# A fused scan, expert and gated-layer kernel: silu's table load placed earlier, and work in later stages re-spaced

## The chip, the cores and the metric

The kernel runs on one core of a Trainium2 chip. The metric is the device time of one execution in microseconds (us). Engines are named as in the profile: PE (TensorE matmul), PEld (its weight loads), DVE (VectorE), ACT (ScalarE), POOL (GpSimd), SP (SyncE, which issues the DMAs).

## What is computed

A chunked linear scan gives 3072 tokens of 256 features. A mixture of 4 experts with normalised weights follows, and then one gated layer with silu:

```python
x = scan(x, a, B, C)                     # 3072 x 256 tokens
p = domain_probs / (domain_probs.sum(-1, keepdims=True) + 1e-09)
out = np.zeros((N, D), dtype=np.float32)
for e in range(E):                       # E = 4, F = 1024
    h = np.maximum(x @ w1[e], 0.0)
    out += p[:, e:e + 1] * (h @ w2[e])
g = out @ w_gate                         # d_ff = 1536
silu = g * (1.0 / (1.0 + np.exp(-g)))
val = out @ w_val
return (silu * val @ w_out)
```

## The kernel before

Every fp32 product is made of rounded parts: a value is split into a high and a low part, and three matmuls (high by high, low by high, high by low) take the place of one. A plain 128x512 product therefore shows as three rows on PE (or as two rows, one of them x2). The suffixes h and l in tile names are these parts. `high` (L702 in the trace) is ACT's copy that rounds, `low` (L705) is the subtraction on POOL that leaves the rest.

The work has four stages, and PE goes through them in one written order.

- **Scan, with experts 0 and 1 for the first 2048 tokens**, to 223 us. Slots 0 to 159 of about 1.3 us each hold half of one token tile's product with one block of w1 and w2; the scan's steps are put between them.
- **Eight blocks of the other experts' work**, 223 to 550 us. From slot 160 (`n0`) on, eight blocks of 1024 tokens, each an expert and a pair p of token tiles: `blocks = [(2, 0), (2, 2), (2, 1), (0, 2), (1, 2), (3, 0), (3, 1), (3, 2)]`. A block has four quads, a quad four slots of some 2.55 us. A block whose expert is new has its four quads' weights prepared during the block before, which is 12 quads, from about 346 to 450 us. A quad is a 2x2 block product in the manner of Strassen, with seven products instead of eight: `expert_hidden` writes the banks X, Y, Z, W in the order X A11, Y S2, W S3, Z S1, X A12, Y A22, Z S4. After X A11 ACT copies X into Y, after Y S2 it copies Y into Z (L1032, L1035), after W S3 and Z S1 it saves W and Z into SBUF (`c<-d` L1037, `c<-h` L1040), and `out` rounds the four results (L1026). `expert_project` (L1078) multiplies them by w2 two slots or more later. Operands are sums of token tiles (`token_sums`: s1, s2, s3 on POOL at L862, with the copies t3h and t24h on ACT) and sums of weight blocks (`gate_sums`, L713 to L716, on POOL).
- **The gated layer**, 550 to 813 us, in 18 steps; step i has `dense_gate(i)` and `dense_value(i)` with the same seven products each. The gate ends in silu on ACT (L1132 through `scopy`), the value multiplies it in on DVE. `plain_product` (L985, tile `dr`) and `side_product` are the products with w_out; `plain()`, `side_product` and `before(...)` stand in the functions `fill_a` and `fill_b`, which are called between products.
- **The tail**, 813 us to the end: the last products with w_out in the order of the list `order`, added on DVE (L1281) and stored from SP and ACT.

Where the work stands is set by hand. `put(slot, fn)` and `job(steps, slots)` hang a step on a slot, `spread(seq, a, b)` spaces a sequence evenly between two slots, `quad(i, j, h)` is the slot of block i, quad j, part h. At each slot PE's products are written first into the program, and the steps of that slot are written behind them, on whatever engine they use. Each engine works through its instructions in that order. So a step at an earlier slot stands further ahead in the queue of its engine; it also blocks what is behind it if its operands are late.

`expert_quad(e, j)` prepares the weights of one quad in seven steps: `load` (two DMAs from SP into `raw_q`), `high_a` and `low_a` (the first three blocks), `sums`, `high_s` (two copies on ACT), `low_s`, `low_o`. `dense_tokens(p)` makes the token sums of a pair p in six steps (i0, i1, s2, i3, s4, s5), where i3 is s3 and the copy t3h. `expert_tokens` does the same ahead of the experts. `dense_quad` turns the gated layer's weights into parts in the same way, by way of DVE and stores to DRAM. `share_load` fetches the mixture weights of a block, `hidden_load` the weights of one gated step. The last products of the last expert block (`parts`, project 21 among them) are done inside step 0 of the gated layer, by `before(...)`.

ACT has one function table at a time. In the program an `ACT_TABLE_LOAD` stands ahead of the first silu.

## Time and profile before

| what | value |
| --- | --- |
| time, median of 3 runs | 823.12 us (822.6 to 823.57) |
| the profiled execution | 823.93 us |
| its span | 822.2 us |
| PE busy | 812.7 us, 99% of the span, 4361 matmuls |
| DVE, ACT, POOL busy | 564.8, 549.2, 504.7 us |
| granted TensorE clock | 1.00 of full speed (the 2.4 GHz level) in all 40 slices |
| DMA | 129.06 MB, 157 GB/s on average |

The profiled execution has 1.7 us around its span and is 0.8 us above the median. In the timelines a row has the start, the duration, the engine, the line, the operation, output<-inputs, and in brackets the idle time of that engine before it with what ended it (given from about 0.15 us on). A matmul row lasts 0.39 us while its successor starts 0.227 us later, because matmuls overlap; a matmul that comes after a pause is 0.50 us long.

### The profile page before, as it was taken

Reading aid. Unit: us, or ns where it says so; the run is one execution under the profiler, and the core shown is the slowest. Engines: PE = TensorE matmul, PEld = TensorE weight load, DVE = VectorE, ACT = ScalarE, POOL = GpSimd, SP = SyncE. Lnnn points to the kernel's source line nnn. Section 1 sums busy time; section 2 is a strip of 40 time slices with the busy share of each in tenths; the row PEclk is TensorE's granted clock in tenths of the full one; section 3 lists DMA queues with packets and bytes.
Section 4 is the critical chain, followed back from the end, with each engine's and each line's share of the span. In section 5 each row is a group of like instructions: output and inputs, shape, how many; then the busy total and the mean of one; then the engine's idle time right before and its main releaser. Section 6 shows DMA issues by size and latency. Waiting matters only on the chain.

```text
span 822.2 us, 12888 instructions
## 1 busy us (share of the span) xinstructions
PE 812.7 (99%) x4361; PEld 671.6 (82%) x4361; DVE 564.8 (69%) x861; ACT 549.2 (67%) x1109; POOL 504.7 (61%) x527
## 2 busy tenths in 40 slices
PE   8999999999999999999999999999999999999998
PEld 7998888888778888888888888887787888888886
DVE  6877668555257756565756574736889878877777
ACT  6687776666366565767776666546577677677763
POOL 4764775434399533777897347513688568847752
PEclk9999999999999999999999999999999999999999
DMA  8864545541301336344443242363555366637651
GB/s 272 281 233 144 170 148 193 194 165 65 105 25 48 119 97 208 116 153 142 145 160 96 92 145 94 137 237 93 174 189 194 109 249 229 225 121 269 226 165 51
DMA packets 67218, 129.06 MB, mean 157 GB/s; under 512 B 6288, under 2 KB 34512, under 8 KB 67152
## 3 DMA queue, kind: packets, MB, share of 16 engines
q1 hardware_dynamic: 67008, 128.11, 46.7%
q8 instruction: 34, 0.56, 0.3%
q14 instruction: 32, 0.26, 0.1%
q10 hardware_dynamic: 144, 0.13, 0.0%
HBM read 108.41 MB, written 19.81 MB: 156 GB/s over the span
## 4 chain that ended last, share of the span: by engine, by line
PE 94%; POOL 2%; ACT 2%; DVE 1%; issue 1%; DVEq 0%; ACTq 0%; POOLq 0%
PE h L958 31%; PE h L631 11%; PE d L1078 10%; PE po L1078 10%; PE po L639 10%; PE d L958 7%; PE d L985 6%; PE o L985 3%; PE ypsum L546 1%; PE scores L475 1%; PE h L985 1%; PE ypsum L491 1%; POOL acc L862 1%; POOL xl L705 0%; PE ypsum L504 0%
## 5 line engine op out<-in xcount | busy, mean ns | idle before, releaser
L1043 DVE TENSOR_TENSOR d<-d,c 128x512 f32<-128x512 f32 x32 | 22.3, 698 | 104.1 <-ACT c L1040 104.1
L673 DVE SCALAR_TENSOR_TENSOR hl<-h,hh 128x512 fp32r<-128x512 f32 (+1 forms) x80 | 46.5, 582 | 58.9 <-ACT hh L672 58.7
L1078 PE MATMUL po<-hh,we_o 128*128 128x512 f32 x256 | 78.9, 389 | 0.5 <-DVE acc L694 0.5
L1078 PE MATMUL d<-hh,we_o 128*128 128x512 f32 x256 | 78.9, 389 | 0.0
L1027 DVE SCALAR_TENSOR_TENSOR hl<-h,hh 128x512 fp32r<-128x512 f32 x96 | 65.9, 688 | 18.2 <-PE d L1078 12.1
L672 ACT ACTIVATE hh<-h 128x512 fp32r<-128x512 f32 (+1 forms) x80 | 40.5, 508 | 55.2 <-PE h L631 54.9
L1026 ACT ACTIVATE hh<-h 128x512 fp32r<-128x512 f32 x96 | 57.0, 596 | 25.7 <-DVE h L1047 22.6
L433 ACT ACTIVATE L<-L,cum 128x128 f32<-128x128 f32 x176 | 56.1, 394 | 3.7 <-POOL L L426 3.7
L958 PE MATMUL h<-xh,wq_h 128*128 128x512 f32 x144 | 56.6, 393 | 0.6 <-ACT xh L1132 0.6
L631 PE MATMUL h<-xh,w_h 128*128 128x512 f32 (+1 forms) x160 | 56.3, 352 | 0.7 <-POOL Bw L461 0.7
L639 PE MATMUL po<-hh,w_h 128*128 128x512 f32 (+1 forms) x160 | 56.3, 352 | 0.6 <-DVE tmp L692 0.6
L1078 PEld LDWEIGHTS po<-hh,we_o 128*128 128x128 f32 x256 | 48.0, 188 | 10.8 <-ACT we_o L702 0.9
L631 PE MATMUL h<-xh,w_l 128*128 128x512 f32 (+1 forms) x160 | 55.8, 349 | 0.4 <-DVE w_l L275 0.4
L1078 PEld LDWEIGHTS d<-hh,we_o 128*128 128x128 f32 x256 | 48.1, 188 | 10.0
L958 PE MATMUL h<-xh,wq_l 128*128 128x512 f32 x144 | 56.1, 389 | 0.0
L958 PE MATMUL h<-xl,wq_h 128*128 128x512 f32 x144 | 56.1, 389 | 0.0
L639 PE MATMUL po<-hl,w_h 128*128 128x512 f32 (+1 forms) x160 | 55.6, 348 | 0.0
L639 PE MATMUL po<-hh,w_l 128*128 128x512 f32 (+1 forms) x160 | 55.5, 347 | 0.0
L631 PE MATMUL h<-xl,w_h 128*128 128x512 f32 (+1 forms) x160 | 55.5, 348 | 0.0
L958 PE MATMUL h<-xh,we_h 128*128 128x512 f32 x128 | 50.0, 391 | 0.4 <-ACT c L1040 0.3
L958 PE MATMUL h<-xh,we_l 128*128 128x512 f32 x128 | 49.8, 389 | 0.0
L1078 PE MATMUL po<-hl,we_o 128*128 128x512 f32 x128 | 49.8, 389 | 0.0
(489 smaller groups left out, 2540.6 us busy)
## 6 DMA issues: line engine op xcount, KB each, us to landing
wq_h<-wd_d SPq DMA_DIRECT2D x36, 448.0 KB
wq_l<-wd_d SPq DMA_DIRECT2D x36, 448.0 KB
L<-crow_d SPq DMA_DIRECT2D x22, 512.0 KB
bc<-in_bc_dram SPq DMA_DIRECT2D x21, 512.0 KB
wq_o<-wp_d SPq DMA_DIRECT2D x24, 384.0 KB
raw_q<-in_w_dram SPq DMA_DIRECT2D x32, 256.0 KB
wq_s<-ws_d SPq DMA_DIRECT2D x18, 384.0 KB
pbc<-probs_d SPq DMA_DIRECT2D x22, 256.0 KB
```

The costliest lines, as they stand in the source:

```text
L433: nc.scalar.activation(out=L[:, h, :], in_=L[:, h, :], func=AF.Exp, bias=cols(cum, q)[:, h:h + 1])
L475: nc.tensor.matmul(ps[:, 2 * g:2 * g + 2, :], r["Bs"][:, 2 * half + g, :], r["Cs"][:, 2 * half + g], start=(g == 0), stop=True, skip_group ...
L631: nc.tensor.matmul(ps, w[:, k, fs], v[:, k, :], start=(i == 0), stop=(i == len(ops) - 1))
L639: nc.tensor.matmul(po[d], w[:, fc, dsl], x, start=(first and i == 0), stop=(last and i == 2))
L672: nc.scalar.activation(out=hh, in_=ph, func=AF.Relu)
L673: nc.vector.scalar_tensor_tensor(out=hl, in0=ph, scalar=0.0, in1=hh.bitcast(F32), op0=ALU.max, op1=ALU.subtract)
L958: nc.tensor.matmul(ps, x[:, ws], y, start=(start and i == 0), stop=(i == 2), skip_group_check=True)
L985: nc.tensor.matmul(ps[:, z:z + n], x, y[:, z:z + n], start=(start and i == 0), stop=(stop and i == 2), skip_group_check=True)
L1026: S.activation(out=hh, in_=ps, func=AF.Relu)
L1027: return lambda: V.scalar_tensor_tensor(out=hl, in0=ps, scalar=0.0, in1=hh.bitcast(F32), op0=ALU.max, op1=ALU.subtract)
L1043: V.tensor_tensor(out=W, in0=W, in1=v, op=ALU.add)
L1078: nc.tensor.matmul(po[d], both[:, z, dsl], y, start=(first and i == 0), stop=(last and i == 2), skip_group_check=True)
```

## The change

Five things change.

1. In gate 0 of the gated layer, behind the copy of X into Y, a silu of one column of a new tile `probe` is written; the program then has its `ACT_TABLE_LOAD` there. `probe` is 32 columns wide (128 bytes per partition) and is set to zero by DVE at the very start.
2. In step 1 of the gated layer, and ahead of it: the fourth of the `parts` moves from value 0 (between W S3 and X A12) into gate 1 behind X A11, and the plain product that stood there moves behind gate 1's Y S2.
3. Steps of `expert_quad(2, j)` come one or two slots earlier (base 138, 146, 154, 161 becomes 136, 145, 153, 160); `dense_tokens(2)` gets fixed slots n0 + 0, 1, 2, 3, 5, 6; the tokens of experts 0 and 1 get written slots in place of an even spread; a number in `PAIRS` goes from 1.1 to 1.2.
4. In the blocks of experts 2 and 3, `load` of the next expert's quad comes one slot later (offset 2 instead of 1) and `high_a` one slot earlier (3 instead of 4); `share_load` comes one slot earlier, one `dense_quad` one slot later, `dense_tokens(0)` about two slots earlier, `hidden_load` of step 0 a few slots later.
5. In the tail, `order` has 17 ahead of 22 instead of behind it.

On ACT, around gate 0, the program had this; L1121 is the copy of X into Y, the first L1132 row the copy of Y into Z, `ds<-d` and `ds<-h` save W and Z, and `xh<-h` is the first silu:

```order
L1121 ACTIVATE h_6215<-h_6214 128x512
L1132 ACTIVATE h_6216<-h_6215 128x512
L1132 ACTIVATE ds_6195<-d_6217 128x512
L1132 ACTIVATE ds_6196<-h_6216 128x512
L1132 ACT_TABLE_LOAD
L1132 ACTIVATE xh_6202<-h_6214 128x512
L1132 ACTIVATE ds_6197<-ds_6197 128x512
```

and has this after the change:

```order
L1123 ACTIVATE h_6217<-h_6216 128x512
L1134 ACT_TABLE_LOAD
L1134 ACTIVATE probe<-probe 128x1
L1134 ACTIVATE h_6218<-h_6217 128x512
L1134 ACTIVATE ds_6197<-d_6219 128x512
L1134 ACTIVATE ds_6198<-h_6218 128x512
L1134 ACTIVATE xh_6204<-h_6216 128x512
L1134 ACTIVATE ds_6199<-ds_6199 128x512
```

The load and the probe stand between the two bank copies; the silus follow the saving copies directly.

On PE, in gate 1, the program had this from the last product of value 0 on (`d<-t24h` is W A22, `h<-xh` is X A11 of gate 1, `d<-dr` the plain product, `h<-t24h` Y S2):

```order
L958 MATMUL d_6271<-t24h_92,wq_h 128x512
L958 MATMUL d_6271<-t24h_92,wq_l 128x512
L958 MATMUL d_6271<-t24l_93,wq_h 128x512
L958 MATMUL h_6339<-xh_78,wq_h 128x512
L958 MATMUL h_6339<-xh_78,wq_l 128x512
L958 MATMUL h_6339<-xl_82,wq_h 128x512
L985 MATMUL d_6351<-dr_6190,wq_o 128x512 x2
L985 MATMUL d_6351<-dr_6191,wq_o 128x512
L958 MATMUL h_6340<-t24h_92,wq_h 128x512
L958 MATMUL h_6340<-t24h_92,wq_l 128x512
L958 MATMUL h_6340<-t24l_93,wq_h 128x512
```

and has this after the change, from X A11 of gate 1 on (`po` is project 21 of the last expert block):

```order
L960 MATMUL h_6336<-xh_78,wq_h 128x512
L960 MATMUL h_6336<-xh_78,wq_l 128x512
L960 MATMUL h_6336<-xl_82,wq_h 128x512
L1080 MATMUL po_5943<-hh,we_o 128x512 x2
L1080 MATMUL po_5943<-hl,we_o 128x512
L1080 MATMUL po_5944<-hh,we_o 128x512 x2
L1080 MATMUL po_5944<-hl,we_o 128x512
L960 MATMUL h_6337<-t24h_93,wq_h 128x512
L960 MATMUL h_6337<-t24h_93,wq_l 128x512
L960 MATMUL h_6337<-t24l_94,wq_h 128x512
L987 MATMUL d_6362<-dr_6192,wq_o 128x512 x2
L987 MATMUL d_6362<-dr_6193,wq_o 128x512
```

Project 21 stood 10 rows ahead of the first row shown of before, in front of X A12 of value 0; it has taken the plain product's place, which now comes after Y S2.

On POOL, at the start of expert 2, the program had this (`raw_q<-raw_q` are the four operations of `sums` of quad 2, `acc` the token sums, `xl` and `we_l` lower parts):

```order
L705 TENSOR_TENSOR we_l<-raw_q,we_h 128x384
L705 TENSOR_TENSOR xl_3057<-acc_91,xh_3055 128x512
L713 TENSOR_TENSOR raw_q<-raw_q 128x128
L714 TENSOR_TENSOR raw_q<-raw_q 128x128
L715 TENSOR_TENSOR raw_q<-raw_q 128x128
L716 TENSOR_TENSOR raw_q<-raw_q 128x128
L862 TENSOR_TENSOR acc_91<-acc_91 128x512
L705 TENSOR_TENSOR xl_3056<-acc_90,xh_3054 128x1024
L862 TENSOR_TENSOR acc_91<-acc_91,acc_90 128x512
L862 TENSOR_TENSOR acc_90<-acc_91,acc_90 128x512
L705 TENSOR_TENSOR we_l<-raw_q,we_h 128x512
L705 TENSOR_TENSOR we_o<-raw_q,we_o 128x512
```

and has this after the change:

```order
L707 TENSOR_TENSOR we_l<-raw_q,we_h 128x384
L715 TENSOR_TENSOR raw_q<-raw_q 128x128
L716 TENSOR_TENSOR raw_q<-raw_q 128x128
L717 TENSOR_TENSOR raw_q<-raw_q 128x128
L718 TENSOR_TENSOR raw_q<-raw_q 128x128
L707 TENSOR_TENSOR xl_3059<-acc_91,xh_3057 128x512
L864 TENSOR_TENSOR acc_91<-acc_91 128x512
L707 TENSOR_TENSOR xl_3058<-acc_90,xh_3056 128x1024
L707 TENSOR_TENSOR we_l<-raw_q,we_h 128x512
L864 TENSOR_TENSOR acc_91<-acc_91,acc_90 128x512
L864 TENSOR_TENSOR acc_90<-acc_91,acc_90 128x512
L707 TENSOR_TENSOR we_o<-raw_q,we_o 128x512
```

The four sums stand ahead of the lower part `xl` of the tokens, and the weights' `we_l` ahead of the pair of token sums.

The whole diff:

```diff
--- before.py
+++ after.py
@@ -87,6 +87,7 @@
     bacc = [xpool.tile([P, KD, BN], F32, name=f"acc{i}", tag=f"acc{i}") for i in range(NBLK)]
     xh, xl, acc = ([v[o // BN][:, :, o % BN:o % BN + n] for o, n in zip(offs, sizes)] for v in (bxh, bxl, bacc))
     T = {}
+    probe = xpool.tile([P, 32], F32, name="probe", tag="probe")
 
     def token_tiles(pool, p):
         T[p] = [[pool.tile([P, KD, BN], F32R, name=f"t24{z}_{p}", tag=f"t24{z}_{p}") for z in "hl"],
@@ -124,6 +125,7 @@
         nc.gpsimd.affine_select(out=t, in_=src, pattern=pattern, base=base, channel_multiplier=cm, compare_op=op, fill=0.0)
 
     def constants():
+        nc.vector.memset(probe, 0.0)
         nc.vector.memset(ones, 1.0)
         nc.vector.memset(lower, -1e4)
         keep(upto, ones, [[1, P]], 0, -1)
@@ -1357,7 +1359,7 @@
             return n0 + (i * NQE + j) * 4 + h
 
 
-        PAIRS = [(0, 0, 28), (0, 0, 46), (0, 0, 60), (6.3, 1.1, 72.5), (6.8, 0.9, 85), (4.3, 1, 95), (4.3, 0.8, 103), (5.8, 1, 117), (5.8, 1.1, 129), (6.8, 1.1, 141), (4.3, 1, 151)]
+        PAIRS = [(0, 0, 28), (0, 0, 46), (0, 0, 60), (6.3, 1.1, 72.5), (6.8, 0.9, 85), (4.3, 1, 95), (4.3, 0.8, 103), (5.8, 1, 117), (5.8, 1.1, 129), (6.8, 1.2, 141), (4.3, 1, 151)]
 
         SLOTS = {
             4: (22, 24, 25, 26, 28, 29, 35),
@@ -1441,23 +1443,23 @@
         put(11, lambda: pair_loads(4))
 
         seq, t1 = expert_tokens(0, bacc[4], bacc[5])
-        spread(seq, 72, 100)
-        put(102, t1)
+        for step, slot in zip(seq + [t1], (72, 76, 80, 86, 90, 94, 98, 104), strict=True):
+            put(slot, step)
 
         def job(steps, at):
             for fn, a in zip(steps, at, strict=True):
                 put(a, fn)
 
-        for j, a in enumerate((138, 146, 154, 161)):
+        for j, a in enumerate((136, 145, 153, 160)):
             job(expert_quad(2, j), [a + o for o in (0, 4, 5, 7, 8, 9, 10)])
         for i in range(1, len(blocks)):
             e = blocks[i][0]
             if e == blocks[i - 1][0]:
                 continue
             for j in range(NQE):
-                job(expert_quad(e, j), [quad(i - 1, j) + o for o in (1, 4, 5, 6, 12, 13, 14)])
+                job(expert_quad(e, j), [quad(i - 1, j) + o for o in (2, 3, 5, 6, 12, 13, 14)])
         for i, (e, p) in enumerate(blocks):
-            put(quad(i, 2, 1), lambda e=e, p=p: share_load(e, p))
+            put(quad(i) + 8, lambda e=e, p=p: share_load(e, p))
 
         tpool = None
 
@@ -1474,10 +1476,10 @@
             banks.extend((dpools["ps"], f"d{i}") for i in range(3))
 
         cctx = ExitStack()
-        spread(dense_tokens(2), n0, quad(0, 2))
+        job(dense_tokens(2), [n0 + o for o in (0, 1, 2, 3, 5, 6)])
         seq, t1 = expert_tokens(1, bacc[4], bacc[5])
-        spread(seq + [t1], quad(0, 2), quad(1, 2))
-        starts = [2, 6, 14, 22, 26, 34, 38, 46, 54, 58, 66, 70, 78, 86, 90, 98, 102, 110]
+        job(seq + [t1], [n0 + o for o in (8, 10, 12, 14, 16, 18, 20, 22)])
+        starts = [2, 6, 14, 22, 26, 34, 38, 46, 54, 58, 66, 71, 78, 86, 90, 98, 102, 110]
         for z, start in enumerate(starts):
             at = n0 + start
             for fn, gap, parts in dense_quad(*divmod(z, 3)):
@@ -1485,8 +1487,8 @@
                 while (at - n0) % 4 not in parts or parts is SUMS and (at - n0) % (4 * NQE) in (3, 4):
                     at += 1
                 put(at, fn)
-        spread(dense_tokens(0), quad(6, 1, 3), quad(7, 2))
-        put(quad(7, 1, 3), lambda: (hidden_load(0, 0), hidden_load(0, 1)))
+        job(dense_tokens(0), [n0 + o for o in (101, 103, 106, 109, 112, 115)])
+        put(n0 + 121, lambda: (hidden_load(0, 0), hidden_load(0, 1)))
 
         def at(*key):
             for fn in todo.pop(key, []):
@@ -1563,7 +1565,9 @@
                 if i == 0:
                     before(parts[2 * what])
                 elif what == 0:
-                    if i > NQD or i == 1:
+                    if i == 1:
+                        before(parts[3])
+                    if i > NQD:
                         plain()
                     if i > 1:
                         side_product(i - 2, T3)
@@ -1575,8 +1579,11 @@
                     fn()
                 late.clear()
                 if i == 0:
-                    before(parts[2 * what + 1])
+                    if what == 0:
+                        before(parts[1])
                 elif what == 0:
+                    if i == 1:
+                        plain()
                     if i > 1:
                         side_product(i - 2, T2)
                     if full:
@@ -1589,6 +1596,8 @@
             def gate(h):
                 if h == 0:
                     flush()
+                    if i == 0:
+                        scopy(probe[:, :1], probe[:, :1], AF.Silu)
                     if i > 0:
                         if i > NQD:
                             side_split(i - 1, T1)
@@ -1660,7 +1669,7 @@
         p, n = NPAIR - 1, len(quads)
         rounded.extend(v for part in operand_tiles(p, F32R) for v in cells(*part))
         flush()
-        order[:] = [(p, k) for k in (4, 6, 7, 8, 9, 10, 5, *range(12, 17), 11, *range(18, 23), 17, 23)]
+        order[:] = [(p, k) for k in (4, 6, 7, 8, 9, 10, 5, *range(12, 17), 11, *range(18, 22), 17, 22, 23)]
         to_split[:] = [pk for pk in order if pk in to_split]
         loads_ahead(24)
         side_split(n - 1, T1, nc.vector)
```

## Rows read from the trace of the kernel before

**Rows 1.** Page, part 4: shares of the chain that ended last, by engine.

```profile
PE 94%; POOL 2%; ACT 2%; DVE 1%; issue 1%; DVEq 0%; ACTq 0%; POOLq 0%
```

**Rows 2.** Waits of PE over the span: us in total, times, longest us.

```profile
PE h L631 <- POOL Bw L461: 0.7, 1, 0.7
```

**Rows 3.** Windows, blocks 1 to 7: us, busy us (x instructions), clock, DMA.

```profile
243.00:531.00 288.00, 288.00 (x1271) 238.28 (x1270) 187.42 (x283) 189.36 (x344) 187.08 (x224) 1.00 0.38 125
```

**Rows 4.** Timeline of ACT, gate 0: start, us, engine, line, tiles, idle before.

```profile
551.31 0.58 ACT L1121 ACTIVATE h<-h 128x512 f32<-128x512 f32 x1 [1.38 <-PE h L958]
553.35 0.58 ACT L1132 ACTIVATE h<-h 128x512 f32<-128x512 f32 x1 [1.46 <-PE h L958]
...
556.68 1.28 ACT L1132 ACT_TABLE_LOAD   x1
557.98 0.60 ACT L1132 ACTIVATE xh<-h 128x512 f32<-128x512 f32 x1
```

**Rows 5.** Timeline of PE, gate 0 into value 0.

```profile
555.19 0.39 PE L958 MATMUL h<-xh,wq_h 128*128 128x512 f32 x1
...
558.63 0.50 PE L958 MATMUL h<-xh,wq_h 128*128 128x512 f32 x1 [0.56 <-ACT xh L1132]
```

**Rows 6.** Timeline of PE, value 0 through gate 1.

```profile
562.88 0.61 PE L1078 MATMUL po<-hh,we_o 128*128 128x512 f32 x2
...
567.94 0.50 PE L985 MATMUL d<-dr,wq_o 128*128 128x512 f32 x1 [0.37 <-POOL dr L705]
...
573.54 0.50 PE L958 MATMUL h<-xh,wq_h 128*128 128x512 f32 x1
```

**Rows 7.** Timelines of DVE and POOL, value 0 into gate 1.

```profile
563.03 0.69 DVE L1129 TENSOR_TENSOR ds<-h,ds 128x512 f32<-128x512 f32 x1 [1.21 <-ACT ds L1132]
...
565.12 0.69 DVE L1129 TENSOR_TENSOR xh<-h,xh 128x512 f32<-128x512 f32 x1 [0.59 <-PE h L958]
...
566.61 1.28 POOL L705 TENSOR_TENSOR dr<-xh,dr 128x512 fp32r<-128x512 f32 x1 [2.95 <-issue]
```

**Rows 8.** Timelines of POOL, ACT and PE, first block of expert 2.

```profile
226.32 1.29 POOL L705 TENSOR_TENSOR xl<-acc,xh 128x512 fp32r<-128x512 f32 x1 [2.52 <-ACT xh L702]
227.57 0.46 POOL L713 TENSOR_TENSOR raw_q<-raw_q 128x128 f32<-128x128 f32 x1
...
233.22 2.65 POOL L862 TENSOR_TENSOR acc<-acc,acc 128x512 f32<-128x512 f32 x2
...
238.31 1.32 POOL L862 TENSOR_TENSOR acc<-acc 128x512 f32<-128x512 f32 x1
...
234.54 0.58 ACT L1032 ACTIVATE h<-h 128x512 f32<-128x512 f32 x1 [0.86 <-DVE hl L1027]
...
239.66 0.63 ACT L702 ACTIVATE t24h<-acc 128x512 fp32r<-128x512 f32 x1 [1.20 <-POOL acc L862]
...
241.31 0.58 ACT L1040 ACTIVATE c<-h 128x512 f32<-128x512 f32 x1
...
235.18 0.50 PE L958 MATMUL h<-t24h,we_h 128*128 128x512 f32 x1 [0.15 <-ACT h L1032]
...
241.94 0.50 PE L958 MATMUL h<-xh,we_h 128*128 128x512 f32 x1 [0.34 <-ACT c L1040]
```

**Rows 9.** DMA view of 379 to 400 us, and timelines of SP and ACT there.

```profile
DMA  0475799999910002998930004994000000025766
...
379.72 0.39 SPq L726 DMA_DIRECT2D raw_q<-in_w_dram  x1
...
389.73 0.52 ACT L702 ACTIVATE we_h<-raw_q 128x384 fp32r<-128x384 f32 x1
```

**Rows 10.** Timelines of DVE and ACT's queue, the end.

```profile
817.40 0.69 DVE L1281 TENSOR_TENSOR xh<-h,xh 128x512 f32<-128x512 f32 x1 [1.27 <-PE h L985]
818.11 0.76 DVE L1281 TENSOR_TENSOR acc<-d,acc 128x256 f32<-128x256 f32 x2
...
818.90 0.37 ACTq L1242 DMA_DIRECT2D out_dram<-acc  x1
```

## The prediction

> **What bounds the kernel now.** I read the shares of the chain that ended last first: PE holds 94% of it [rows 1]. The clock is granted in full, so nothing is to be had there. Next I read the windows: from 243 to 531 us PE is busy for 288.00 of 288.00 us, with 1271 matmuls, one per 288.00 / 1271 = 0.2266 us [rows 3]. This is the pace. There is no gap in this stretch, so a moved step can win nothing there; it can only create a wait. What can be won are PE's own pauses outside it. A matmul after a pause is 0.50 us long instead of 0.39 [rows 5], so each pause costs some 0.11 more behind it. A pause is therefore the start of its matmul, less the start of the one before, less 0.2266, plus 0.11. The change aims at three pauses (at 242, 558 and 567 to 574 us) and at the end of the tail. I sum against the profiled execution, 823.93 us, and take the difference off the median, 823.12.
>
> **The table load.** Before, ACT loads the table at 556.68 for 1.28 us, and the first silu runs at 557.98 to 558.58 [rows 4]. Value 0's first product writes the bank that this silu reads, and starts at 558.63, after 0.56 idle [rows 5]; the matmul before it ended at 558.07, so it began at 557.68, and at the pace this one would have begun at 557.91. The pause is 0.72, with the restart 0.83. After the change the load follows the copy of 551.31 to 551.89 and lies in ACT's idle 1.46 us before the next copy at 553.35 [rows 4]. It ends at 551.89 + 1.28 = 553.17; the probe, one column, I price below the 0.6 of a full silu and above nothing. Even at 0.6 the copy of Y into Z comes at 553.8 and ends at 554.4, and PE asks for its result only at 555.19 [rows 5]. The silu then runs at 556.68 to 557.28, before 557.91: **gain 0.83**, bounds 0.7 and 0.85. The page "ScalarE: Activation LUTs" of the Trainium skill, section "What ACT_TABLE_LOAD costs", puts a drain of about 1.38 us on top of some 1.28 for the load, 2.66 in all. In this trace the load has its 1.28, but the silu starts 0.02 after it, so no drain is seen. DVE's zeroing of the probe is one small instruction at the start. No row shows one like it; in the first tiles PE waits 0.7 for POOL anyway [rows 2], which covers a delay of DVE, so I take nothing and keep 0.1 either way.
>
> **Project and plain product in step 1.** From 562.88 to 573.54 PE issues 42 matmuls [rows 6]; at the pace they take 9.52 us, the stretch takes 10.66. So 1.14 are pauses: one is the 0.37 idle before the plain product's second matmul at 567.94, which waits for POOL's lower part `dr` [rows 6], started at 566.61 for 1.28 [rows 7]; the others lie before W S3 of gate 1 and before 573.54. After the change, in the clock of before: X A12 takes the project's place at 562.88 and Z S4 would follow at 563.56. Z S4 overwrites the bank that DVE reads from 563.03 to 563.72 [rows 7], so it waits till 563.78, a new pause of 0.22 + 0.11 = 0.33. DVE's next chain starts when X A12 and its factors are done, at about 564.45 instead of 565.12 [rows 7], that is 0.67 earlier, and POOL's `dr` with it: it ends at 566.61 + 1.28 - 0.67 = 567.22. The project fills 1.36 us (6 matmuls), Y S2 another 0.68, and the plain product is reached at about 567.99: no pause. The bank for W S3, which DVE frees 0.67 earlier, is asked for at 568.67, free at 568.41: no pause. The last pause, before 573.54, I leave at 0.17. The stretch ends at 562.88 + 9.52 + 0.33 + 0.17 = 572.90: **gain 0.64**. What it hangs on is DVE's order. If the chain did not start earlier than 565.12, `dr` would come at 567.89, still just ahead, but W S3 would wait some 0.4, restart included: gain 0.2. Bounds 0.1 and 0.75.
>
> **The early respacing.** At 226.32 POOL starts the tokens' lower part, and behind it four sums of 0.46 from 227.57 on, then an unbroken row of work to the third token sum at 238.31 (1.32 us) [rows 8]. ACT's copy t24h waits for that sum till 239.66, and two more ACT instructions lie between it and the copy `c<-h` at 241.31 (three in 1.65, 0.55 each), for which PE waits till 241.94 [rows 8]. At the pace PE would have started at 241.94 - 0.34 - 0.16 = 241.44, so the pause costs 0.50 + 0.11 = 0.61. In the new order the four sums stand ahead of 226.32, in POOL's idle 2.52 us [rows 8]; they need about 2.0. The third token sum then ends at about 239.63 - 2.0 = 237.6, t24h no longer blocks, `c<-h` is done at about 240.4, a microsecond early: gain 0.61. But ACT's order changes too: the copies t3h and `xh`, which need the pair of token sums at 233.22, now stand ahead of the bank copy at 234.54 [rows 8]. The pair loses the sums' 2.0 but gains the weights' lower part ahead of it (1.3), so its first half (1.33 of 2.65) ends at 233.22 - 0.7 + 1.33 = 233.85. Two copies at 0.55 put the bank copy at 234.95 instead of 234.54, and PE's wait for it, in the row at 235.18 [rows 8], grows by some 0.35. **Gain 0.61 - 0.35 = 0.26**, bounds 0.6 and -0.15. The other moves of this part (token sums of experts 0 and 1, loads and splits in slots 136 to 160) stand where PE has no pause; there I take 0 with 0.2 either way.
>
> **The middle.** Nothing to win. For each of the 12 quads whose weights are prepared there the load comes one slot (2.55) later and the rounding copy `high_a` one slot earlier. Before, at 379.72, a load is issued and its copy runs at 389.73; by the DMA row, in slices of 0.525 us, the queues are busy from there to about 385.3, with a store and another load beside it, and the next load, at 386, takes under 4 us [rows 9]. So 10.0 us become 4.9, if both moves count in full, against 3 to 5.6 for landing. But SP issues when a buffer is free, and this does not move with the slot: counted in matmuls, the instruction that frees the way lies 31 or more ahead of the copy, 7.0 us. **0**, bounds 0 and, at 0.3 for each of 12 quads, a loss of 3.6 (its rival below). The copies for the gated layer's tokens and the later `hidden_load` lie beside PE's unbroken work; 0, with 0.3 of loss as bound.
>
> **The tail.** DVE adds product 17 at 817.40 to 818.09, and only then the two halves of the last product, from 818.11; ACT issues the last store at 818.90 [rows 10]. Product 17 is made 0.68 (three matmuls) earlier after the change, so its add ends at 817.4, and the halves follow PE: the first is done before PE ends, at about 818.07, the second add takes 0.76 / 2 = 0.38 and some 0.1 to start. The last store is issued at about 818.56: **gain 0.34**, bounds 0.2 and 0.4.
>
> Sum: 0.83 + 0.64 + 0.26 + 0.34 = 2.07. 823.93 - 2.07 = 821.86 for a profiled execution, **823.12 - 2.07 = 821.0 us** for the median, 0.25% less.
>
> **The rivals.** What a measurement of this kernel can tell from no change is about 0.2%, here 1.65 us.
>
> First, the moved work gives back what it gains. Gate 1's waits are bank handovers between PE and DVE, and DVE is nearly unbroken from 565 on; the early part has an ACT queue with a new wait at its head. If both end at nothing, table and tail remain: 823.12 - 0.83 - 0.34 = 821.95, within 0.2%. For it: two of the four terms rest on when a queue of another engine is free, to 0.3 us. Against it: the waits that go are named in the rows.
>
> Second, slower: the weight loads come late. Place: `high_a` at the head of ACT's queue in the 12 quads, ahead of the copy of X into Y, which PE wants some 0.8 us after it can start. It decides when a load needs more than 7.0 us from its release, or when SP is held by a store ahead of it. At 8.1 us PE would wait about 0.3 in each quad, with the restart 0.4: 4.8 us, so 821.0 + 4.8 = 825.8. The longest landing that I read is 5.6 [rows 9], so this is unlikely.
>
> Third, the change doesn't do what it says: the silus need a further load, because an instruction between the probe and the first silu puts another table in. Then 0.83 stays lost: 821.9, within 0.2%. Against it: in the new order only copies lie between them, and in the trace copies follow silus with no further load.
>
> Fourth, the load holds ACT for longer than its row. PE's product of 555.19 [rows 5] decides: the copy before it takes 0.58 and PE follows 0.05 behind, so load and probe have from 551.89 to 554.56, 2.67 us, twice the load's 1.28 and a little. At 2.75 PE would start 0.08 late, 0.19 with the restart: 821.2, still faster. Against it: the silu at 557.98 follows its load by 0.02 [rows 4]. The drain of the Trainium skill's page "ScalarE: Activation LUTs" would be such a case.
>
> **How the numbers follow.** Forecast 0.55, the longer load 0.03: both faster. The gains given back 0.28, the further load 0.05: within 0.2%. Late loads 0.06, and 0.03 for small new pauses in the middle that add up beyond the gain: slower. Of the forecast's cases the sum can end below 1.65 where both the moves stay near their lower bounds, which is the first rival. So faster 0.58, same 0.34, slower 0.08. Low end: all terms at their upper bounds, 0.85 + 0.75 + 0.6 + 0.4 = 2.6, with 0.4 from the small unknowns: 820.1. High end: the first rival with 0.7 for new pauses: 822.7.
>
> **What would show it.** Table: a load at 551.9 on ACT, and value 0's first product at the pace. Step 1: no idle before the plain product, a short one before Z S4, gate 1 over about 0.6 earlier. Early: POOL's sums ahead of `xl`, PE without a pause before Z S4 of quad 1 but with a longer one before Y S2. Middle: 1271 matmuls in 288.0 us, as before. Tail: the add of 17 ahead of PE's end. I would be wrong if PE showed pauses between 250 and 550, or if gate 1's pauses moved on to value 1 with the same sum.

## The result and the profile after

The changed kernel takes **828.03 us** (median of 5 runs, 826.65 to 828.42) against 823.12 (5 runs, 822.6 to 823.95): ratio 1.0055, 95% interval 1.0041 to 1.0069. It is slower by 4.9 us where 2.1 us less were forecast, and outside the range (820.1 to 822.7).

The profiled execution took 827.52 us, with a span of 825.8. The fence has, of the changed kernel, the page's shares of the chain, the window of [rows 3], and three rows of PE's list of waits (us in total, times, longest).

```profile
PE 92%; POOL 3%; issue 2%; ACT 2%; DVE 1%; DMA 1%; DVEq 0%; POOLq 0%; SPq 0%; ACTq 0%
...
243.00:531.00 288.00, 288.00 (x1263) 236.59 (x1262) 184.99 (x279) 187.59 (x341) 185.80 (x223) 1.00 0.37 119
...
PE h L633 <- POOL Bw L463: 0.7, 1, 0.7
...
PE po L1080 <- DVE acc L696: 0.4, 1, 0.4
...
PE h L960 <- DVE ds L1131: 0.3, 1, 0.3
```

The chain is PE's as in [rows 1], and the clock is granted in full as in [rows 3]. The two waits that the change aims at, for `xh` at value 0 and for `dr` at the plain product, are gone from the list ([rows 5] and [rows 6] have them, 0.56 and 0.37), and the longest that has come in is the 0.3 for `ds`. PE is busy for 288.00 of 288.00 us, as before. But it has done 1263 matmuls in them and not 1271: one per 288.00 / 1263 = 0.2280 us, not 0.2266. **Nobody waits, and yet each matmul comes later.** Eight matmuls fewer are 8 x 0.2266 = 1.8 us in this stretch alone.

Which matmuls are they? The next view groups PE's instructions in 437 to 500 us (experts' blocks whose tokens are those of pairs 0 and 1), with busy us, mean ns of one and idle time before it. The first fence is of the kernel before, the second of the changed one.

```profile
L958 PE MATMUL h<-xh,we_h 128*128 128x512 f32 x25 | 9.7, 389 | 0.0
...
L958 PE MATMUL h<-xl,we_h 128*128 128x512 f32 x25 | 9.7, 389 | 0.0
```

```profile
L1080 PE MATMUL po<-hh,we_o 128*128 128x512 f32 x50 | 15.5, 392 | 0.0
...
L960 PE MATMUL h<-xl,we_h 128*128 128x512 f32 x25 | 9.9, 397 | 0.0
L960 PE MATMUL h<-xh,we_h 128*128 128x512 f32 x25 | 9.9, 394 | 0.0
...
L960 PE MATMUL h<-t24h,we_h 128*128 128x512 f32 x12 | 4.7, 391 | 0.0
...
L960 PE MATMUL d<-t3h,we_h 128*128 128x512 f32 x6 | 2.3, 389 | 0.0
```

Before, each of the five forms has a mean of 389 ns there. After, those whose moving tile is `xl` or `xh` have 397 and 394, `po<-hh` 392, `t24h` 391, `t3h` still 389. The starts tell the same: the mean distance from one 128x512 matmul to the next (distances under 330 ns, worked out from the timeline of this stretch) was 226.67 ns and is 229.49. The distances were 226 or 227 throughout; now they run from 223 to 239.

The steps of the forecast can still be found. The timelines of ACT and PE in the first block of expert 2, of ACT and PE at gate 0 to value 1, and of DVE and ACT's queue at the end (start, us, engine, line, tiles, idle before):

```profile
240.57 0.59 ACT L1042 ACTIVATE c<-h 128x512 f32<-128x512 f32 x1
...
242.50 0.40 PE L960 MATMUL h<-xh,we_h 128*128 128x512 f32 x1
...
553.67 0.58 ACT L1123 ACTIVATE h<-h 128x512 f32<-128x512 f32 x1 [1.40 <-PE h L960]
554.27 1.28 ACT L1134 ACT_TABLE_LOAD   x1
555.56 0.20 ACT L1134 ACTIVATE probe<-probe 128x1 f32<-128x1 f32 x1
555.74 0.58 ACT L1134 ACTIVATE h<-h 128x512 f32<-128x512 f32 x1
...
560.36 0.39 PE L960 MATMUL h<-xh,wq_h 128*128 128x512 f32 x1
...
564.97 0.40 PE L960 MATMUL h<-xl,wq_h 128*128 128x512 f32 x1
565.40 0.50 PE L960 MATMUL h<-xh,wq_h 128*128 128x512 f32 x1
...
566.20 0.50 PE L960 MATMUL d<-t24h,wq_h 128*128 128x512 f32 x1
...
574.79 0.50 PE L960 MATMUL h<-xh,wq_h 128*128 128x512 f32 x1
...
820.69 0.69 DVE L1283 TENSOR_TENSOR xh<-h,xh 128x512 f32<-128x512 f32 x1 [0.78 <-PE h L987]
822.08 0.75 DVE L1283 TENSOR_TENSOR acc<-d,acc 128x256 f32<-128x256 f32 x2 [0.69 <-PE d L987]
...
822.86 0.37 ACTq L1244 DMA_DIRECT2D out_dram<-acc  x1
```

Against [rows 8], PE no longer pauses before Z S4 (242.50, no idle) since `c<-h` now runs at 240.57. Against [rows 4, 5], the load stands at 554.27, and value 0's first product (560.36) follows at the pace. Against [rows 6], there is no wait for `dr`; the pauses left are those before 565.40, 566.20 and 574.79. Against [rows 10], product 17's add starts 1.39 ahead of the halves, not right before them. All that was aimed at is there. The loss lies beside it.

### The profile page after: what moved, and what is told of

Read it like the earlier page. It is cut to its first block, busy times and chain, and to the rows that moved or that the text cites. A ratio compares the mean times of both kernels' runs of the same rounds, so it can differ in the third digit from the quotient of the medians.

```text
span 825.8 us, 12893 instructions
## 1 busy us (share of the span) xinstructions
PE 817.6 (99%) x4361; PEld 671.5 (81%) x4361; DVE 562.6 (68%) x862; ACT 550.6 (67%) x1110; POOL 506.8 (61%) x527
## 4 chain that ended last, share of the span: by engine, by line
PE 92%; POOL 3%; issue 2%; ACT 2%; DVE 1%; DMA 1%; DVEq 0%; POOLq 0%; SPq 0%; ACTq 0%
PE h L960 32%; PE d L1080 11%; PE po L1080 10%; PE h L633 9%; PE po L641 9%; PE d L960 7%; PE d L987 6%; PE o L987 3%; PE ypsum L548 1%; PE h L987 1%; PE scores L477 1%; PE ypsum L493 1%; DMA L<-crow_d 1%; POOL L L428 1%; POOL acc L864 0%
## 5 line engine op out<-in xcount | busy, mean ns | idle before, releaser
L960 PE MATMUL h<-xl,we_h 128*128 128x512 f32 x128 | 50.3, 393 | 0.0
```

The source lines that it names most:

```text
L960: nc.tensor.matmul(ps, x[:, ws], y, start=(start and i == 0), stop=(i == 2), skip_group_check=True)
```

## The experiments

The theory after this reading: the 128 bytes of the probe, put into the middle of the first pool, move every buffer behind it, so that a matmul's weights and its moving tile no longer lie alike, and this costs pace. The rivals: the new order of the work costs it (DMAs and other engines in other places), or the early table load does.

What moves, by the addresses in the built programs (bytes per partition): `xh` and `xl` of pairs 0 and 1 and `acc` stand ahead of the probe and stay (`xh0` at 1152). `t24h` of pair 0 goes from 58496 to 58624, the first weight buffer from 70784 to 70912, and with them all other weights, the hidden parts and pair 2's tokens. Before, all of these were at 128 modulo 256. After, weights are at 0 and the tokens `xh`, `xl` of pairs 0 and 1 at 128.

### Shift alone, and all but the shift

`e1_shift_only` is the kernel before with only the tile and its zeroing:

```diff
     T = {}
+    probe = xpool.tile([P, 32], F32, name="probe", tag="probe")
 ...
     def constants():
+        nc.vector.memset(probe, 0.0)
```

> The kernel before with the tile probe of 128 bytes in the place where the changed kernel has it, zeroed once, and nothing else changed. In the changed kernel PE's waits went as forecast in several places, yet its matmuls lost the even pace: from 600 to 700 us the mean distance of two 128x512 matmuls is 230.5 ns, before 227.2 ns. Theory A, the 128 bytes: all buffers behind the probe (weights, rounded hidden parts, half of the tokens) move by 128 bytes, and matmuls are slowed by that. Then this kernel is slower than before by the lost pace, some 5 to 7 us: about 829, and 600 to 700 us holds about 432 matmuls instead of 438. Theory B, the moved work: the lost pace comes from instructions that run beside the matmuls at other times. Then this kernel is at 823, with 438 matmuls.

`e2_after_no_shift` is the changed kernel with these two lines taken out and the probe put last into the last pool, so that no buffer moves:

```diff
         free.extend(dpool.tile([P, BN], F32, name=f"ds{i}", tag=f"ds{i}") for i in range(3))
+        probe = dpool.tile([P, 32], F32, name="probe", tag="probe")
+        nc.vector.memset(probe, 0.0)
```

> The changed kernel with the probe as the last tile of the gated layer's last pool, where no other buffer moves; DVE zeroes it there. Theory A: the even pace is back and the forecast gains stay: 820.5 to 821.5. Theory B: as the changed kernel, 826 to 828, with matmuls at 230 ns from 600 to 700 us.

Measured: e1 828.45 us against 823.31, ratio 1.0058 (1.0044 to 1.0072). e2 821.66, ratio 0.9979 (0.9969 to 0.9989). The window, the products with `xl` in 437 to 500, and one row of expert 2's first block, of e1:

```profile
243.00:531.00 288.00, 288.00 (x1263) 236.62 (x1263) 185.84 (x280) 188.17 (x342) 188.06 (x224) 1.00 0.38 125
...
L960 PE MATMUL h<-xl,we_h 128*128 128x512 f32 x24 | 9.5, 396 | 0.0
...
242.71 0.50 PE L960 MATMUL h<-xh,we_h 128*128 128x512 f32 x1 [0.23 <-ACT c L1042]
```

And of e2 the window, the same products, ACT in expert 2's first block, PE in gate 1, and DVE and ACT's queue at the end:

```profile
243.00:531.00 288.00, 288.00 (x1270) 237.97 (x1269) 186.91 (x281) 188.98 (x343) 185.44 (x223) 1.00 0.38 122
...
L958 PE MATMUL h<-xl,we_h 128*128 128x512 f32 x25 | 9.7, 389 | 0.0
...
233.46 0.62 ACT L702 ACTIVATE t3h<-acc 128x512 fp32r<-128x512 f32 x1
234.52 0.63 ACT L702 ACTIVATE xh<-acc 128x512 fp32r<-128x512 f32 x1 [0.44 <-POOL acc L862]
235.19 0.58 ACT L1032 ACTIVATE h<-h 128x512 f32<-128x512 f32 x1
...
240.20 0.60 ACT L1040 ACTIVATE c<-h 128x512 f32<-128x512 f32 x1
...
562.69 0.39 PE L958 MATMUL h<-xl,wq_h 128*128 128x512 f32 x1
563.13 0.50 PE L958 MATMUL h<-xh,wq_h 128*128 128x512 f32 x1
...
563.94 0.50 PE L958 MATMUL d<-t24h,wq_h 128*128 128x512 f32 x1
...
572.43 0.50 PE L958 MATMUL h<-xh,wq_h 128*128 128x512 f32 x1
...
817.40 0.76 DVE L1281 TENSOR_TENSOR acc<-d,acc 128x256 f32<-128x256 f32 x2 [0.70 <-PE d L985]
...
818.19 0.37 ACTq L1242 DMA_DIRECT2D out_dram<-acc  x1
```

One unused tile costs the whole loss: e1 has 1263 matmuls in the window and 396 ns on `xl`, as the changed kernel has, while it keeps the old order (the pause at 242.71 is still there). e2 has 1270 and 389, and is faster than before. So **the shift costs 5.1 us, and the rest of the change gains 1.65**. By matmuls of the same count in the traces of before and e1, the loss builds up by 1.1 from the 1200th (134 us) to the 1800th (231 us), 1.8 to the 3180th (546 us), 2.2 to the 4200th (782 us) and 0.25 to the end, 5.4 in all; the first 1200 vary by 1 us from one execution to the next. It is spread over the program, with no place where it happens. In the changed kernel the shift costs as much: from the 1200th matmul on, its trace falls 5.3 behind that of e2, which does the same work in the same order.

### The early silu alone

`e3_silu_no_shift` is the kernel before with the probe at the end, as in e2, and

```diff
                 if h == 0:
                     flush()
+                    if i == 0:
+                        scopy(probe[:, :1], probe[:, :1], AF.Silu)
```

> The kernel before with the early silu alone, its probe where no other buffer moves. Theory A and the forecast's first term: 0.8 us less than before, 822.3, PE's pause of 0.56 us before value 0 gone. Theory B: the same, since no work is moved; a slower pace here would speak against both.

Measured: 822.73 us, ratio 0.9993 (0.9984 to 1.0002). ACT at gate 0, and PE's first product of value 0:

```profile
551.33 1.28 ACT L1132 ACT_TABLE_LOAD   x1
552.63 0.20 ACT L1132 ACTIVATE probe<-probe 128x1 f32<-128x1 f32 x1
552.77 0.58 ACT L1132 ACTIVATE h<-h 128x512 f32<-128x512 f32 x1
...
557.34 0.39 PE L958 MATMUL h<-xh,wq_h 128*128 128x512 f32 x1
```

The product follows at the pace. By the starts of the same matmul in the two traces, 0.84 us is won there. The timed difference, 0.58 with an interval from a gain of 1.3 to a loss of 0.2, holds that and doesn't prove it; the rows do. The load takes 1.28, the probe starts 0.02 after its end and takes 0.20, and the next copy starts 0.14 behind the probe's start. The Trainium skill's page "ScalarE: Activation LUTs", section "What ACT_TABLE_LOAD costs", puts a drain of about 1.38 us on top of the load; no run here shows it, neither behind the load nor ahead of it (in the changed kernel it starts at 554.27, 0.02 after the copy of 553.67 ends).

### Which buffers, and how far

If positions decide, then moving everything together must cost nothing, and moving the weights away from all tokens must cost more than the change did. `e5_all_shift` is e2 with 128 unused bytes ahead of all pools (they are zeroed once at the start, like the probe, and so are those of e6 and e7):

```diff
+    padx = ctx.enter_context(tc.tile_pool(name="padx", bufs=1)).tile([P, 32], F32, name="padx", tag="padx")
     xpool = ...
```

> The kernel of run e2 (all of the change, probe at the end) with 128 unused bytes ahead of every buffer: all of them lie at 256 within 512 bytes, none moves against another. The shift of the probe is now known to cost 5 us; what in it does is open. Theory place: buffers at 256 within 512 are slow to read; then this is as slow as the changed kernel, 827, matmuls of 437 to 500 us 229.5 ns apart on average. Theory mix: it needs buffers that lie differently within 512 bytes side by side; then this is as fast as e2, 821 to 822, with 226.7 ns.

`e6_weights_only` is e2 with 128 bytes ahead of the weights' pool and 384 ahead of the next one, the hidden parts' (512 in all, so that only the weights change their place within 256 bytes):

```diff
+    padw = ctx.enter_context(tc.tile_pool(name="padw", bufs=1)).tile([P, 32], F32, name="padw", tag="padw")
     wpool = ...
+    padh = ctx.enter_context(tc.tile_pool(name="padh", bufs=1)).tile([P, 96], F32, name="padh", tag="padh")
     hpool = ...
```

> The kernel of e2 with the weights' pool alone moved by 128 bytes; tokens, hidden parts and all later buffers lie within 512 bytes as before. Theory mix of weights and moving operand (the matmul reads both at once): every product is uneven, in all blocks, 230 ns or more from 437 to 500 us and from 369 to 424 us too, 828 or more. Theory mix of moving operands one after another (tokens, then hidden parts): no product is, since all moving operands lie alike: 226.7 ns, 821 to 822.

`e7_hidden_on` is e2 with 128 bytes ahead of the hidden parts' pool alone. Weights and the first pool stay; hidden parts, pair 2's tokens and pair 1's `t24` and `t3`, which lie behind, move:

```diff
+    padh = ctx.enter_context(tc.tile_pool(name="padh", bufs=1)).tile([P, 32], F32, name="padh", tag="padh")
     hpool = ...
```

> The kernel of e2 with 128 unused bytes behind the weights: hidden parts, mixture weights and the tokens of the last two pairs move, weights and the tokens of pair 0 don't. Theory mix of weights and moving operand: the projections (hidden parts against weights) are uneven in all blocks, the products with tokens of pair 0 are even. Theory mix of moving operands: uneven at the change from tokens to hidden parts, in blocks of pair 0, about as in the changed kernel; in blocks of pair 2, whose tokens move too, even, 226.7 ns.

Then the changed kernel itself, with the probe where it is but of another size: `e4_after_512`, `e8_after_256`, `e9_after_64` and `e10_after_32` move what lies behind it by 512, 256, 64 and 32 bytes.

```diff
-    probe = xpool.tile([P, 32], F32, name="probe", tag="probe")
+    probe = xpool.tile([P, 128], F32, name="probe", tag="probe")
```

That is e4; e8 has 64 columns, e9 16 and e10 8.

> The changed kernel with a probe of 128 columns, 512 bytes, in its place in the changed kernel: later buffers move by 512 bytes instead of 128. Theory A in the form that any move hurts: 827 to 829, uneven pace. Theory A in the form that the position within 512 bytes matters, which is that of before here: about 821, pace 226.7 ns in the expert blocks. Theory B: 827, uneven pace.

> The changed kernel with a probe of 64 columns, 256 bytes, in its place: later buffers move by 256 bytes against the first twelve. Theory mix within 512 bytes: uneven as with 128 bytes, 826 or more. Theory mix within 256 bytes: even, 226.7 ns from 437 to 500 us, 821 to 822.

> The changed kernel with a probe of 16 columns, 64 bytes, in its place. Runs e4, e6 and e8 showed that weights and moving operand 128 bytes apart are slow and 256 or 512 apart are not. Theory period of 256 bytes: what counts is whether both lie alike within 256 bytes; at 64 apart the products with tokens of pairs 0 and 1 are uneven too, 826 to 829. Theory multiples of 64 (any multiple but 128 is harmless, or the slot of 64 bytes alone counts): even, 226.7 ns from 437 to 500 us, 821 to 822.

> The changed kernel with a probe of 8 columns, 32 bytes, in its place, so that later buffers lie at no multiple of 64. Theory period of 256 bytes: uneven about as with 64 or 128 bytes, 826 to 829. Theory multiples of 64: slower than with 64 bytes, above 829, and in blocks of pair 2, where all operands moved, uneven too.

The window of each. e5, everything moved together by 128:

```profile
243.00:531.00 288.00, 288.00 (x1270) 237.71 (x1269) 187.14 (x281) 188.97 (x342) 184.20 (x223) 1.00 0.38 124
```

e6, weights moved alone, with the durations (ns, least, median and greatest) of the products with `xl` in 437 to 500 us:

```profile
243.00:531.00 288.00, 288.00 (x1241) 233.49 (x1240) 179.46 (x275) 186.29 (x337) 182.90 (x222) 1.00 0.36 117
...
L962 PE MATMUL h<-xl,we_h x24: 390/392/404, 439.3 to 497.1; 128*128 128x512 f32 x24
```

e7, hidden parts and all behind them moved:

```profile
243.00:531.00 288.00, 288.00 (x1243) 233.37 (x1242) 179.71 (x276) 186.80 (x338) 182.92 (x222) 1.00 0.36 118
```

The changed kernel with a probe of 512, 256, 64 and 32 bytes:

```profile
243.00:531.00 288.00, 288.00 (x1271) 238.10 (x1270) 187.21 (x281) 189.02 (x343) 185.15 (x223) 1.00 0.38 123
```

```profile
243.00:531.00 288.00, 288.00 (x1271) 237.72 (x1269) 187.10 (x281) 188.95 (x342) 184.22 (x223) 1.00 0.39 124
```

```profile
243.00:531.00 288.00, 288.00 (x1261) 236.13 (x1261) 184.72 (x278) 187.59 (x341) 185.28 (x223) 1.00 0.37 119
```

```profile
243.00:531.00 288.00, 288.00 (x1263) 236.53 (x1262) 185.19 (x279) 188.56 (x342) 187.11 (x224) 1.00 0.37 118
```

With the mean distances from start to start, worked out as above, once in 437 to 500 us (tokens of pairs 0 and 1) and once in 350 to 420 (tokens of pair 2):

| kernel | what lies unlike its weights, modulo 256 bytes | us | 437-500, ns | 350-420, ns |
|---|---|---|---|---|
| before | nothing | 823.1 | 226.67 | 226.67 |
| after (128) | `xh`, `xl` of pairs 0, 1, by 128 | 828.0 | 229.49 | 226.84 |
| e1, shift alone | the same | 828.5 | 229.45 | 226.73 |
| e2, no shift | nothing | 821.7 | 226.67 | 226.85 |
| e5, all moved by 128 | nothing | 821.5 | 226.67 | 226.86 |
| e6, weights moved by 128 | all tokens and hidden parts | 836.8 | 232.41 | 232.37 |
| e7, hidden parts and on moved by 128 | hidden parts, pair 2's tokens, `t24` and `t3` of pair 1 | 833.7 | 231.19 | 232.38 |
| e4, probe of 512 | nothing (512 is twice 256) | 822.5 | 226.67 | 226.77 |
| e8, probe of 256 | nothing | 821.5 | 226.67 | 226.83 |
| e9, probe of 64 | `xh`, `xl` of pairs 0, 1, by 64 | 827.7 | 229.80 | 226.98 |
| e10, probe of 32 | the same, by 32 | 829.2 | 229.37 | 227.19 |

e1, e2, e3 and e5 were timed in several rounds (e5: 821.52, ratio 0.9976, 0.9967 to 0.9986); e4 and e6 to e10 are one run each, which is enough for steps of 5 to 15 us, not to rank e2, e4, e5 and e8. The time of e10, 829.15, lies at the border of its two theories ("826 to 829" and "above 829"); the pace decides, which with 32 bytes is no worse than with 64 (229.37 against 229.80) and stays near 227 in blocks of pair 2.

Three things follow. It is not the bytes, nor the place as such: moved together, everything is as fast as unmoved (e5). It is the weights' place against the moving tile's, and 256 bytes is the period as far as tried: 0, 256 and 512 are even, 32, 64 and 128 are not. So "multiples of 64 bytes" protects nothing; 64 is no better than 32. And the loss goes by how many products are unlike: where pair 2's tokens move with the weights (after, e1), blocks (0,2) and (1,2) in 350 to 420 us keep their pace; where all products are unlike (e6), none has it.

Why a matmul should care stays **open**; since all weight buffers lie alike within 256 bytes, the runs don't even tell whether the weights that a matmul uses count, or those that are loaded beside it. One detail can be read further: in after, `po<-hh` has 392 ns although hidden parts and `we_o` lie alike there. Counted from the last product with `xh` or `xl` in 437 to 500 us, the first five matmuls behind it, whatever their tiles, start their successors 229.1 to 234.6 ns later on average, and from the sixth on it is 226.5 to 226.8. In e1 it is five as well, in e7 three. So the unevenness is carried on for a few matmuls, which is why forms that often come right behind `xl` are touched and `t3h` is not; how it is carried on is open too.

The first stage (100 to 200 us, from a 128x512 matmul to the next matmul of any form) also slowed, from 230.5 to 233.4 ns. By the addresses its products of `xh` and `xl` with w1 go from alike to 128 bytes apart, as in the later blocks, so this fits; but the scan's own tiles lie at several places already before, and no run took the two apart.

### Two parts of the respacing undone

`e11_undo_quads` is e2 with expert 2's quads back at their slots, `e12_undo_project` is e2 with the project and the plain product back in their old places of step 1:

```diff
-    (136, 145, 153, 160)
+    (138, 146, 154, 161)
```

> The kernel of e2 with the quads of expert 2 back at 138, 146, 154 and 161, so that quad 2's sums stand behind the tokens' lower part on POOL again; dense_tokens(2) stays as changed. Theory of the forecast (the sums held up the token sums, t24h and the saving copy): PE's pause of about 0.5 us before Z S4 of quad 1, at 242, is back, 0.6 us slower than e2. Rival (the earlier dense_tokens step did it): no pause there.

```diff
-                    if i == 1:
-                        before(parts[3])
-                    if i > NQD:
+                    if i > NQD or i == 1:
                         plain()
 ...
-                    if what == 0:
-                        before(parts[1])
+                    before(parts[2 * what + 1])
                 elif what == 0:
-                    if i == 1:
-                        plain()
```

> The kernel of e2 with project 21 and the plain product back in their old places. Forecast: PE's idle 0.37 before the plain product and the shorter pause before W S3 come back, the pause before Z S4 goes; from the start of value 0 to value 1, 0.4 to 0.65 us longer than in e2. Rival (bank handovers give the gain back): the same length within 0.1 us.

PE's row in e11 (first block of expert 2) with ACT's copy `xh` there, and PE's row in e12 (gate 1):

```profile
235.94 0.50 PE L958 MATMUL h<-t24h,we_h 128*128 128x512 f32 x1 [0.72 <-ACT h L1032]
...
234.77 0.63 ACT L702 ACTIVATE xh<-acc 128x512 fp32r<-128x512 f32 x1 [0.35 <-POOL acc L862]
```

```profile
566.61 0.50 PE L985 MATMUL d<-dr,wq_o 128*128 128x512 f32 x1 [0.37 <-POOL dr L705]
```

e11 (822.85 us, one run): the pause before Z S4 does not come back. In its place PE waits 0.72 before Y S2, where e2 and before wait 0.15 to 0.17. With `t3h` and `xh` ahead of the bank copy and the four sums ahead of the pair again, POOL is late for `xh` and the bank copy behind it. From the 1800th to the 1920th matmul e11 loses 0.53 on e2, so neither theory is right as it stood: the moved token sums alone end the wait before Z S4, but bring one of the same size before Y S2, and the sums' new place ends that one. Whether the sums' new place alone, with the token sums left, would win the 0.6 by the route of the forecast was not run. e12 (822.25, one run): the wait for `dr`, 0.37, is back as in [rows 6], and from value 0 to value 1 e12 loses 0.50 on e2. That term is the project's and the plain product's place.

## Why the prediction was wrong, point by point

**The step that failed** is the one on the probe: "DVE's zeroing of the probe is one small instruction at the start ... I take nothing and keep 0.1 either way". I costed the instruction and not the tile. A tile in the middle of the first pool moves all buffers behind it, and this was no term, not even one with bounds; it is +5.1 us (e1). None of the four rivals was it either. The slower one put its loss into late weight loads; in the trace, the weights' copies hold up PE once in the 12 quads, by about 0.15 at 389 us in e2, and the loss has no wait at all.

**The middle** "1271 matmuls in 288.0 us, as before" is the sign that fell, with 1263. My other sign, "PE showed pauses between 250 and 550", would have missed it: there is no pause. I had taken the pace of 0.2266 from [rows 3] as a constant of the engine. It belongs to the layout.

**The four terms**, read from e2's trace against that of before, where no shift disturbs them:

| term | forecast | measured | |
|---|---|---|---|
| table load | -0.83 | -0.86 (e3: -0.84) | right, and by the route named |
| project and plain product | -0.64 | -0.47 (e12: +0.50 back) | within the bounds, too large |
| early respacing | -0.26 | -0.63 | just past the upper bound of 0.6 |
| tail | -0.34 | -0.35 | right in size, by another route |

*Project and plain product.* The pause before Z S4 came as forecast (562.69 to 563.13 in e2, that is 0.44 - 0.2266 = 0.22, and 0.11 for the restart). The last pause is 0.17 as left (572.03 to 572.43). But W S3's first product has its bank no more than just in time: 0.50 long at 563.94, so another 0.11, and the products behind these pauses come 0.23 to 0.24 apart for a while, some 0.06 more. The stretch from the project's old place to 572.43 takes 10.19 in e2 (from 562.24), against 10.66 before and 10.02 in the forecast.

*Early respacing.* The 0.61 of the pause was right. The new wait of 0.35 that I set against it did not come. I held both copies back until POOL's pair was done; `t3h` needs only a sum that is ready before, and runs at 233.46 in e2, while only `xh` waits, 0.44, till 234.52. The bank copy at 235.19 stands as it stood in [rows 8] with e2's own start of 0.64 later, and PE waits 0.17 for it, not 0.15. Which operand of a moved copy comes last decides, and I had not looked it up for each of the two.

*Tail.* I let the halves' adds follow PE earlier. They start 0.31 after the last matmul in both traces, since PE is what they wait for (817.40, idle 0.70 for PE, in e2), and the last store is issued at 818.19, as far behind PE as before. What has gone is product 17's store out of the last stores' way. In e2 and in before it is issued at:

```profile
816.73 0.33 SPq L1242 DMA_DIRECT2D out_dram<-xh  x1
```

```profile
818.12 0.33 SPq L1242 DMA_DIRECT2D out_dram<-xh  x1
```

That is 0.36 ahead of the last matmul's start in e2, and 0.33 behind it in before. By the DMA packets in the traces the last one of the stores ends 2.52 after that start, not 3.06, and the span 4.03 after it, not 4.38. All kernels with the new `order` end 4.02 to 4.04 after it, those with the old one (before, e1, e3) 4.28 to 4.42; the order alone was not put back.

Not forecast: a new wait stands at the gated layer's end, here in e2:

```profile
785.76 0.50 PE L958 MATMUL h<-xh,wq_h 128*128 128x512 f32 x1 [0.35 <-DVE ds L1129]
```

It costs 0.37 with its restart. It is in after, e2, e4 and e8 to e11, not in before, e1, e3, e5 to e7 and e12. It waits for DVE, but what decides whether it comes is **open**; e5, with the same order of work as e2, has none. PE's small wait near 133.5 us (0.10 in before, none in e2) is no gain of the change: it is 0.56 in e5 and 0.51 in e3.

The four terms make -2.31, with the new wait and the 0.15 at 389 us about -1.8; from the 1200th matmul on, e2's trace gains 1.69 on that of before. e2 was timed at -1.65 and e5 at -1.95, and -2.07 lies within the intervals of both. So the sum was about right for a kernel without the shift, in part by luck: the 0.37 that the early respacing gave beyond its term covers about half of the 0.69 that the project's shortfall (0.17) and the two waits that I had not foreseen (0.37 and 0.15) cost. Of the rivals, the further table load and the longer load are refuted by the rows at 553.67 to 555.74: only one load, and the next copy 1.47 after its start. That the moved work gives everything back is refuted by e2's trace, where step 1 and the early part gain 1.10, with 0.90 forecast.

The best version measured is the change without its shift: e5 with 821.52 and e2 with 821.66, below both kernels.

## What to carry to other kernels

A new tile is also a change of address for every buffer that its pool and the pools behind it place later: put small tiles last, or give them 256 bytes, and compare where a matmul's weights and its moving tile lie modulo 256 before and after. A loss of pace doesn't show as a wait or as idle time; count the matmuls in a window without gaps. A moved copy must be traced to each of its operands, since the latest one sets its new time.

## What the runs showed of the hardware

- A 128x512 matmul whose weights and moving tile lie at the same place modulo 256 bytes starts 226.67 ns after the one before. Where some products are 32, 64 or 128 bytes off, the mean of 437 to 500 us is 229.4 to 231.2; where all are 128 off, 232.4. The granted clock is 1.00 in all these windows. On this kernel that is 5 to 15 us of 822. Behind such products the next three to five matmuls are uneven too, though their own tiles lie alike (after, e1, e7).
- After a pause of PE the next 128x512 matmul is 0.47 to 0.50 long in these rows instead of 0.39, also where the row shows no idle time before it (566.20 in after, 563.94 in e2).
- The table load takes 1.28 us and the next ACTIVATE starts 0.02 after its end; one of a single column takes 0.20.
